# An S4 convolution block with an MLP: four broadcast mask products, inverse sums moved partly to the matmul accumulator, and a new priority table

## The chip, the cores and the metric

The kernel runs on one core of a Trainium2 chip. The metric is device time in microseconds (us) of one execution; lower is better. The engines are named as in the profile: PE is TensorE's matmul path and PEld its weight loads, DVE is VectorE, ACT is ScalarE, POOL is GpSimd, and SP is the engine whose queue issues nearly all DMA transfers.

## What is computed

The reference is a state-space layer (S4) followed by a channel MLP, both with a layer norm in front and a residual around them. Sequence length L is 2048, width D is 512, 128 states per channel, MLP width 1376; inputs and outputs are bf16.

```python
def _A_ref(u, ...):
    dt = jnp.exp(log_dt)[:, None]
    logdA = dt * (A_re + 1j * A_im);  dB = dt * (B_re + 1j * B_im)
    P = jnp.exp(logdA[:, :, None] * l[None, None, :])
    K = jnp.einsum("dn,dnl,dn->dl", Cc, P, dB).real
    # y = irfft(rfft(pad(u)) * rfft(pad(K))), the first L values
    return y + u * Dskip[None, None, :]
def _B_ref(x, ...):
    h = _gelu(jnp.einsum("bsd,df->bsf", _layernorm(x), w1) + b1)
    return jnp.einsum("bsf,fd->bsd", h, w2) + b2
h  = x + _A_ref(_layernorm(x), ...)
h2 = h + _B_ref(_layernorm(h), ...)
```

## The kernel before

**Staging.** The 512 channels are cut into four groups c = 0 to 3 of 128, and the sequence into two halves b = 0 and 1 of 1024 rows. `tables` builds sines and exponentials of the transition for two groups at a time, `kgen` (L1044) forms the convolution kernel's factors from them, and `kspec` (L1074) turns them with the masked weights `W` into one half of the convolution kernel, sends it through DRAM (`AK_d`, 256 KB out and back in) to change its layout, and transforms it (L1112). `ln1` and `xspec` normalise and transform the input; `xswap` makes a copy with the partition halves exchanged. `inverse` (L1118) multiplies spectra and transforms back. For the first half b = 0 a group has one pair (kernel half 0 with input half 0). For b = 1 it has two pairs, since both kernel halves contribute. `tail` (L1216) adds Dskip and the residual and computes the second layer norm's statistics, and `mlp` (L1262) does the two large matmuls (L1274 and L1292) for 512 rows at a time.

**The inverse.** For each of two blocks of eight frequencies (`fh`) and each of two parts `h` (with the matrices `TP1` and `TP2`), a DVE product of 128x1024 bf16 is made for each pair (L1132) into one of four buffers `PR` used in turn. With two pairs the second product is added to the first on DVE (L1134). The resulting `jobs`, always two, go to PE as 8 matmuls of 128x128 each, accumulated in PSUM (L1142), and the sum is evacuated by ACT or DVE (L439 or L441).

**The weights.** `W` has 7 variants of 4 blocks of 128 columns. Each variant and each group g of 32 columns is `valW` (bf16, 4x32) times one column of the mask `msk` (fp32, one value per partition). L830 does this with one `tensor_scalar` of 128 elements for each of the 28 pairs (v, g); the profile shows it as L504, the line of the helper `TS`. `tensor_tensor` calls through the helper `TT` appear as L511. `kspec` reads all of `W`.

**The order of the work.** Nothing is issued in program order. Every step is added to a list with its engine or engines, an estimated cost, and what it reads and writes. `Sched.run` (L192) then plays the list: it repeatedly takes the engine that can start something first, and on it, among the steps that could start within 0.095606 us of the earliest, the one whose group has the smallest number in the table `PRI` (L89; L282). The window and the table thus decide which ready step an engine takes. Groups are named by stage, half and channel group: `iv11` is the inverse of half 1 and group 1, `tl00` and `ty00` are the statistics and the normalised transpose of the first 512 rows, `mu00` and `md00` their two MLP matmuls, `lx0` the second load of the input, which `tail` adds, `cDW` the step that makes `W`. Where a step may run on two engines the plan also chooses the engine. Four PSUM slots of 128x1024 fp32 are shared by all stages and given out by the same plan.

Of the kernel before, what the change touches and what calls it, by code (L numbers as in the profile page):

```python
# [10 lines left out]
ALU = mybir.AluOpType  # L11
# [5 lines left out]
P = 128  # L17
# [60 lines left out]
def runs_of(idx):  # L78
# [8 lines left out]


PRI = {  # L89
    "ta0": 0, "ks03": 1, "gelu": 2, "iv01": 3, "bd02": 4, "dt": 5, "kt00": 6, "iv03": 7, "ty11": 8, "tp": 9, "tl00": 10, "xs11": 11,  # L90
    "gam": 12, "eA": 13, "xs12": 14, "in": 15, "cDW": 16, "bd01": 17, "x10": 18, "iv11": 19, "u0": 20, "kt01": 21, "zt00": 22, "ks11": 23,
    "kt12": 24, "xin1": 25, "x02": 26, "xin": 27, "u1": 28, "c0": 29, "tl10": 30, "xs13": 31, "x03": 32, "xs01": 33, "xs10": 34, "ks10": 35,
    "iv00": 36, "xs00": 37, "ty00": 38, "tb0": 39, "ty10": 40, "x11": 41, "mu00": 42, "cb": 43, "kt03": 44, "eB2": 45, "zt11": 46, "sa": 47,
    "eB": 48, "bd00": 49, "st": 50, "kg2": 51, "w2": 52, "bd10": 53, "zt02": 54, "tl01": 55, "iv13": 56, "mu01": 57, "bd03": 58, "iv10": 59,
    "ks02": 60, "md01": 61, "zt03": 62, "x00": 63, "iv12": 64, "kg3": 65, "lx1": 66, "trig": 67, "sm": 68, "ks01": 69, "kt02": 70, "sinT": 71,
    "kt13": 72, "zt13": 73, "bd13": 74, "tl11": 75, "kt10": 76, "x01": 77, "kg0": 78, "iv02": 79, "mu10": 80, "tb1": 81, "ks00": 82, "lwt": 83,
    "md10": 84, "ks12": 85, "psi": 86, "ty01": 87, "zt01": 88, "w1": 89, "ln1": 90, "ks13": 91, "xs03": 92, "md00": 93, "x13": 94, "bd11": 95,
    "cB": 96, "kg1": 97, "ln0": 98, "cW": 99, "lx0": 100, "x12": 101, "mu11": 102, "bd12": 103, "zt10": 104, "md11": 105, "zt12": 106, "xs02": 107,
    "ta1": 108, "kt11": 109,
}  # L100


# [45 lines left out]
class Sched:  # L148
# [43 lines left out]
    def run(self, nslots):  # L192
# [72 lines left out]
        while av:  # L265
            while wants and ops[wants[0]].start is not None:
                wants.pop(0)
            fs = sorted((slots[s], s) for s in range(nslots) if taken[s] is None)
            best = {}
            for i in av:  # L270
                o = ops[i]
                need = len(o.new)
                if need > len(fs) or (need and i != wants[0] and len(fs) - need < len(ops[wants[0]].new)):
                    continue
                ts = fs[need - 1][0] if need else 0.0
                for e in o.eng:
                    s = max(free[e], ready(o, e), ts)
                    best.setdefault(e, []).append((s, o.pr, i))
            assert best, "stuck"
            e = min(best, key=lambda q: (min(best[q])[0], ENGS.index(q)))  # L280
            s0 = min(best[e])[0]
            s, _, i = min((c for c in best[e] if c[0] <= s0 + 0.095606), key=lambda c: (c[1], c[2]))  # L282
            o = ops[i]
            av.remove(i)
            c = o.cost[o.eng.index(e)] if len(o.cost) > 1 else o.cost[0]
            if e == "PE":
                if o.new:
                    fill(o, max(free[e], fs[len(o.new) - 1][0]), s)
                c = pecost(s, c, o.mm)
            o.start, o.e = s, e  # L290
            free[e] = s + c
            if o.byts:
                b = max(s + c + 1.3, dma_busy)
                dma_busy = b + o.byts / 218e3
                o.end = dma_busy + 0.7
            else:
                o.end = s + c
            for n, p in enumerate(o.new):
                sl = fs[n][1]
                p.slot = sl  # L300
                taken[sl] = p
            for p in set(o.ps):
                left[p] -= 1
                if left[p] == 0:
                    taken[p.slot] = None
                    slots[p.slot] = o.end + LAT_NEXT[e]
            order.append(o)
            for u in users[i]:
                nd[u] -= 1
                if nd[u] == 0:  # L310
                    av.append(u)
# [18 lines left out]
def kernel(ctx, tc, A_u, A_A_re, A_A_im, A_B_re, A_B_im, A_C_re, A_C_im, A_log_dt, A_Dskip,  # L330
# [34 lines left out]
    W = take(bf16, 7, 4, P)  # L365
# [6 lines left out]
    st = take(f32, 8, 6)  # L372
# [11 lines left out]
    psi = take(f32, 512)  # L384
    gam = take(f32, 512)
# [109 lines left out]
    def TS(o, i, s1, s2, op0, op1=None, n=None, mode=2, psum=False, oap=None, iap=None, extra=(), pr=None, eng="DVE"):  # L495
        r = [i] + [s for s in (s1, s2) if isinstance(s, V)] + list(extra)
        f = lambda s: (s.ap() if isinstance(s, V) else s)
        n = n if n is not None else (o.hi - o.lo) // SZ[o.dt]

        def fn(e):  # L500
            a = oap() if oap else o.ap()
            b = iap() if iap else i.ap()
            if op1 is None:
                dve.tensor_scalar(a, b, f(s1), None, op0)  # L504
            else:
                dve.tensor_scalar(a, b, f(s1), f(s2), op0, op1)
        add("DVE", c_dve(n, mode, psum) + 0.065 * sum(isinstance(q, V) for q in (s1, s2)), fn, r=r, w=[o], pr=pr)

    def TT(o, a, b, op, n=None, mode=1, psum=False, oap=None, aap=None, bap=None, pr=None):
        n = n if n is not None else (o.hi - o.lo) // SZ[o.dt]  # L510
        add("DVE", c_dve(n, mode, psum), lambda e: dve.tensor_tensor(oap() if oap else o.ap(), aap() if aap else a.ap(), bap() if bap else b.ap(), op), r=[a, b], w=[o], pr=pr)  # L511
# [131 lines left out]
    msk = ct(f32, 29)  # L643
# [14 lines left out]
    for z in range(2):  # L658
        for r in range(2):
            TT(BD[z], valB, mB, ALU.mult, n=64, oap=lambda z=z, r=r: BD[z].ap().rearrange("p f r g -> p r g f")[:, r], aap=lambda r=r: valB.ap()[:, r].unsqueeze(1).to_broadcast([P, 4, 16]),  # L660
               bap=lambda z=z: mB.ap()[:, 4 * z:4 * z + 4].unsqueeze(2).to_broadcast([P, 4, 16]))
# [163 lines left out]
        TS(DD, valD, mD[g:g + 1], None, ALU.mult, n=32, oap=lambda g=g: DD.ap()[:, :, :, g])  # L825
    valW = ct(bf16, 4, 32)
    AC(valW, codW, ACT.Sin, scale=SINSC, oap=lambda: valW.ap().rearrange("p a b -> p (a b)"), iap=lambda: low16(codW), tbl=True)
    for v in range(7):
        for g in range(4):
            TS(W[v], valW, msk[4 * v + g:4 * v + g + 1], None, ALU.mult, n=128, mode=4, oap=lambda v=v, g=g: W[v].ap()[:, :, 32 * g:32 * g + 32])  # L830

    for f0 in range(0, 16, 4):
        for half, TPx in ((0, TP1), (1, TP2)):
# [284 lines left out]
    def inverse(b, c, pairs, zt, nz):  # L1118

        S.pr = f"iv{b}{c}"  # L1120
        z = Z[nz % 2]
        for fh in range(2):
            f0 = 8 * fh
            p = Ps()
            jobs = []
            for h, TPx in ((0, TP1), (1, TP2)):
                acc = None
                for kf, Xp in pairs:
                    x = Xp[h]
                    pr_ = PR[npr[0] % 4]  # L1130
                    npr[0] += 1
                    add("DVE", c_dve(1024, 2), lambda e, kf=kf, x=x, pr_=pr_, f0=f0: dve.tensor_tensor(pr_.ap(), kf[f0:f0 + 8].ap(), x[f0:f0 + 8].ap(), ALU.mult), r=[kf[f0:f0 + 8], x[f0:f0 + 8]], w=[pr_])  # L1132
                    if acc is not None:
                        add("DVE", c_dve(1024, 2), lambda e, acc=acc, pr_=pr_: dve.tensor_tensor(acc.ap(), acc.ap(), pr_.ap(), ALU.add), r=[acc, pr_], w=[acc])  # L1134
                    else:
                        acc = pr_
                jobs.append((acc, TPx))

            def fn(e, p=p, jobs=jobs, f0=f0):
                for k in range(8):  # L1140
                    for n, (q, TPx) in enumerate(jobs):
                        pe.matmul(pst(p)[:, 128 * k:128 * k + 128], lhsT=q.ap()[:, k, :], rhs=TPx[f0 + k].ap(), start=(n == 0), stop=(n == len(jobs) - 1))  # L1142
            add("PE", 0.44 * len(jobs), fn, r=[q for q, _ in jobs] + [TP1, TP2], w=[p], new=[p], mm=8 * len(jobs))
            evac(lambda z=z, f0=f0: z.ap()[:, :, f0:f0 + 8], lambda p=p: pst(p).rearrange("d (f q) -> d q f", f=8), 1024, [p], [z])
        S.pr = f"zt{b}{c}"
        if b == 1:
            dmat(lambda: zt.ap(), lambda: z.ap().rearrange("d q f -> d (q f)"), [z], [zt])
            return
        p = Ps()

        def tfn(e, p=p):
            for s in range(16):
                pe.transpose(pst(p, bf16)[:, 128 * s:128 * s + 128], z.ap()[:, 8 * s:8 * s + 8, :].rearrange("d q f -> d (q f)"), identb.ap())
        add("PE", 0.88, tfn, r=[z, identb], w=[p], new=[p], mm=16)

        def zfn(e, p=p):
            o, i = zt.ap().rearrange("p s d -> p (s d)"), pst(p, bf16)
            if e == "ACT":
                act.copy(o, i)
            else:  # L1160
                dve.tensor_copy(o, i)
        add(("DVE", "ACT"), (c_dve(2048, 2), c_act(2048)), zfn, r=[p], w=[zt])
# [222 lines left out]
```

## Time and profile before

| what | value |
|---|---|
| median of 8 runs | 279.17 us (277.72 to 283.0) |
| the profiled execution | 279.54 us, of which its span is 277.7 us |
| PE busy | 234.5 us (84% of the span) |
| DVE busy | 210.9 us (76%) |
| ACT busy | 198.5 us (71%) |
| POOL busy | 11.6 us (4%) |
| mean granted PE clock | 0.937 |
| DMA traffic | 30.07 MB |

The span runs from the first to the last instruction of the profiled execution; 1.84 us of that execution's own time lie outside it. Times below are counted from the start of the span. A group row gives the busy time of a group of instructions, the mean duration of one in ns, and the idle time of the engine ahead of them with what ended it. Durations of neighbouring instructions on one engine overlap, so the distance from one start to the next is shorter than a duration.

### The profile page before, as it was taken

The page shows a single profiled execution, that of the slowest core. Times are in us where ns is not written, and L with a number is a line of the kernel's source. Part 1 is how long each engine was busy: PE and PEld are TensorE (multiplying, and loading weights), DVE is VectorE, ACT ScalarE, POOL GpSimd, SP SyncE. Part 2 cuts the span into 40 slices and gives each one's busy share as a digit, 9 for nine tenths or more (in the row PEclk, how much of TensorE's full clock was granted, in tenths as well). Part 3 has the DMA queues.
Part 4 walks back from the last instruction along what each step waited for, and adds up shares of the span by engine and source line. Part 5 has one row for each costly group of instructions (what it writes and reads, how often), then busy time and mean ns, then how long its engine had stood idle before and what let it go on. Part 6 is the DMA issues. An engine that isn't in the chain of part 4 may idle for free.

```text
span 277.7 us, 7867 instructions
## 1 busy us (share of the span) xinstructions
PE 234.5 (84%) x3266; PEld 143.7 (52%) x3282; DVE 210.9 (76%) x499; ACT 198.5 (71%) x230; POOL 11.6 (4%) x136
## 2 busy tenths in 40 slices
PE   6498459688779998759998978679999999999993
PEld 2372124325366754647977865454664444444441
DVE  7899999999964997985669999999970598612011
ACT  2899999989997898145887996998956414841700
POOL 8410000000000000000000000000000000000000
PEclk9999597958999996897999997999999999999999
DMA  6360661043002089878977989976055002002002
GB/s 138 71 152 27 202 170 22 0 130 81 2 2 82 13 156 242 192 197 213 228 189 198 222 190 238 212 181 114 0 105 105 19 21 57 0 2 58 20 24 53
DMA packets 41240, 30.07 MB, mean 108 GB/s; under 512 B 29971, under 2 KB 37492, under 8 KB 40948
## 3 DMA queue, kind: packets, MB, share of 16 engines
q1 hardware_dynamic: 39476, 29.05, 44.3%
q10 hardware_dynamic: 1728, 0.52, 0.9%
q8 instruction: 25, 0.41, 0.6%
q14 instruction: 11, 0.09, 0.1%
HBM read 15.27 MB, written 8.00 MB: 84 GB/s over the span
## 4 chain that ended last, share of the span: by engine, by line
PE 47%; DVE 21%; ACT 18%; issue 6%; DMA 5%; SPq 1%; POOL 0%; DVEq 0%; ACTq 0%; POOLq 0%
PE ps L1292 13%; PE ps L1274 13%; ACT ar L439 5%; DVE ar L441 4%; PE ps L1142 3%; ACT ar L987 3%; PE ps L1058 3%; PE ps L1098 3%; DVE ar L959 3%; DVE ar L504 3%; PE ps L1059 3%; ACT ar L798 3%; DVE ar L511 2%; DMA ar<-AK_d 2%; DVE ar L965 2%
## 5 line engine op out<-in xcount | busy, mean ns | idle before, releaser
L439 ACT CAST ar<-ps 128x1024 bf16<-128x1024 f32 (+2 forms) x67 | 62.7, 986 | 25.2 <-PE ps L1059 8.4
L1276 ACT ACTIVATE ar<-ps,ar 128x512 bf16<-128x512 f32 (+1 forms) x44 | 29.8, 686 | 23.0 <-PE ps L1274 16.6
L1274 PE MATMUL ps<-ar 128*128 128x512 bf16 (+1 forms) x172 | 40.1, 379 | 0.6 <-ACT ar L439 0.3
L1292 PE MATMUL ps<-ar 128*128 128x512 bf16 (+1 forms) x169 | 39.6, 379 | 0.3
L1294 DVE TENSOR_TENSOR ar<-ps,ar 128x512 bf16<-128x512 f32 x16 | 11.0, 690 | 37.2 <-PE ps L1292 37.2
L441 DVE CAST ar<-ps 128x1024 bf16<-128x1024 f32 (+3 forms) x25 | 27.0, 1106 | 10.4 <-PE ps L1059 4.2
L987 ACT ACTIVATE ar<-ps 128x1024 bf16<-128x1024 int16 x36 | 34.3, 1051 | 0.4 <-DVE ar L965 0.4
L1132 DVE TENSOR_TENSOR ar<-ar 128x1024 bf16<-128x1024 bf16 x48 | 31.2, 683 | 0.9 <-PE ps L1142 0.8
L1274 PEld LDWEIGHTS <-ar 128*128 128x128 bf16 (+1 forms) x176 | 17.3, 100 | 20.1 <-issue 0.8
L1292 PEld LDWEIGHTS <-ar 128*128 128x128 bf16 (+1 forms) x176 | 16.9, 98 | 19.1
L511 DVE TENSOR_TENSOR ar<-ar 128x4 f32<-128x4 f32 (+5 forms) x73 | 21.2, 316 | 1.1
L1059 PE MATMUL ps<-ar 128*20 128x33 bf16 x512 | 19.3, 248 | 3.2 <-issue 3.1
L1058 PE MATMUL ps<-ar 128*20 128x33 bf16 x512 | 19.2, 250 | 1.6 <-DVE ar L965 1.3
L1059 PEld LDWEIGHTS <-ar 128*20 128x20 bf16 x512 | 17.6, 126 | 4.3 <-issue 4.3
L1058 PEld LDWEIGHTS <-ar 128*20 128x20 bf16 x512 | 17.1, 124 | 3.7 <-DVE ar L965 1.8
L1142 PE MATMUL ps<-ar 128*128 128x128 bf16 x256 | 16.9, 223 | 1.3 <-ACT ar L439 1.3
L965 DVE TENSOR_TENSOR ar<-ar 128x1024 bf16<-128x1024 bf16 x26 | 17.4, 682 | 0.3
L1142 PEld LDWEIGHTS <-ar 128*128 128x128 bf16 x256 | 15.7, 100 | 3.3 <-issue 0.8
L1031 PE MATMUL ps<-ar 128*32 128x512 f16 x200 | 13.4, 381 | 2.5 <-ACT ar L987 1.3
L1353 PE MATMUL ps<-ar 128*128 128x512 bf16 x28 | 12.3, 566 | 3.7 <-ACT ar L732 2.3
L896 ACT COPY ar<-ps 128x2048 bf16<-128x2048 bf16 x7 | 13.2, 1887 | 2.3 <-PE ps L918 2.3
L1098 PE MATMUL ps<-ar 20*128 20x256 bf16 (+1 forms) x448 | 12.7, 257 | 2.5 <-issue 1.5
(95 smaller groups left out, 370.9 us busy)
## 6 DMA issues: line engine op xcount, KB each, us to landing
AK_d<-ar SPq DMA_DIRECT2D x16, 256.0 KB
ar<-AK_d SPq DMA_DIRECT2D x16, 256.0 KB
ar<-ar SPq DMA_DIRECT2D x16, 256.0 KB
ar<-in_A_u_dram SPq DMA_DIRECT2D x4, 512.0 KB
ar<-in_A_u_dram SPq DMA_DIRECT2D x8, 256.0 KB
out_dram<-ar SPq DMA_DIRECT2D x32, 64.0 KB
ar<-in_B_w_dram SPq DMA_DIRECT2D x4, 344.0 KB
ar<-in_B_w_dram SPq DMA_DIRECT2D x10, 128.0 KB
```

Of the source, the lines that this page charges most:

```text
L439: act.copy(out_fn(), in_fn())
L441: dve.tensor_copy(out_fn(), in_fn())
L511: add("DVE", c_dve(n, mode, psum), lambda e: dve.tensor_tensor(oap() if oap else o.ap(), aap() if aap else a.ap(), bap() if bap else b.ap( ...
L965: add("DVE", c_dve(1024, 2), lambda e: dve.tensor_tensor(ent(e0, lo, 4, rv), ent(e0, lo, 4, rv), Cx(), ALU.mult), r=rE + [sc[1]], w=rE)
L987: add("ACT", c_act(1024), lambda e, p=p, kp=kp: act.activation(sc.ap()[:, :, 2 * kp:2 * kp + 2, :], pst(p).bitcast(i16).rearrange("p (k s ...
L1058: pe.matmul(o, lhsT=Ar.ap()[:, :, d], rhs=Br.ap()[:, :, d], start=True, stop=False, tile_position=(0, 32 * g))
L1059: pe.matmul(o, lhsT=Ai.ap()[:, :, d], rhs=Bi.ap()[:, :, d], start=False, stop=True, tile_position=(0, 32 * g))
L1132: add("DVE", c_dve(1024, 2), lambda e, kf=kf, x=x, pr_=pr_, f0=f0: dve.tensor_tensor(pr_.ap(), kf[f0:f0 + 8].ap(), x[f0:f0 + 8].ap(), ALU. ...
L1142: pe.matmul(pst(p)[:, 128 * k:128 * k + 128], lhsT=q.ap()[:, k, :], rhs=TPx[f0 + k].ap(), start=(n == 0), stop=(n == len(jobs) - 1))
L1274: pe.matmul(pst(p)[:fs, 512 * z:512 * z + 512], lhsT=w1s[dc].ap()[:, fc * P:fc * P + fs], rhs=ybuf.ap()[:, dc, :], start=(dc == 0), stop=( ...
L1276: add("ACT", c_act(512, 1), lambda e, p=p, z=z, fc=fc, fs=fs: act.activation(hT.ap()[:fs, fc, :], pst(p)[:fs, 512 * z:512 * z + 512], ACT. ...
L1292: pe.matmul(pst(p)[:, 512 * z:512 * z + 512], lhsT=hT.ap()[:fs, fc, 128 * t:128 * t + 128], rhs=w2s[fc].ap()[:fs], start=(fc == 0), stop=( ...
```

## The change

Three things are changed.

The 28 scalar products that make `W` become four broadcast products, one for each of the four column blocks `tl`: `valW[tl]` is broadcast over variants and groups, and the mask over the 32 columns, with 896 elements in each.

In `inverse`, the sum over pairs stays on DVE only for the groups c = 2 and 3. For c = 0 and 1 each product becomes a job of its own. For b = 1 this gives four jobs in place of two, and so 32 matmuls in place of 16 in each block of eight frequencies; the DVE additions are not issued. For b = 0 there is one pair, and nothing changes.

The priority table is replaced by another one for the same 110 groups, and the window goes from 0.095606 to 0.084764 us. Some of the entries, before and after: `ty00` 38 and 11, `tl00` 10 and 20, `iv10` 59 and 43, `iv11` 19 and 36, `iv12` 64 and 59, `iv13` 56 and 7, `iv00` 36 and 85, `iv01` 3 and 81, `iv02` 79 and 88, `iv03` 7 and 4, `lx0` 100 and 2, `mu00` 42 and 73, `cDW` 16 and 14, `tb0` 39 and 55.

```diff
-            s, _, i = min((c for c in best[e] if c[0] <= s0 + 0.095606), key=lambda c: (c[1], c[2]))
+            s, _, i = min((c for c in best[e] if c[0] <= s0 + 0.084764), key=lambda c: (c[1], c[2]))
...
-    for v in range(7):
-        for g in range(4):
-            TS(W[v], valW, msk[4 * v + g:4 * v + g + 1], None, ALU.mult, n=128, mode=4, oap=lambda v=v, g=g: W[v].ap()[:, :, 32 * g:32 * g + 32])
+    for tl in range(4):
+        TT(W, valW, msk, ALU.mult, n=896, oap=lambda tl=tl: W.ap()[:, :, tl].rearrange("p v (g i) -> p v g i", g=4),
+           aap=lambda tl=tl: valW.ap()[:, tl].unsqueeze(1).unsqueeze(1).to_broadcast([P, 7, 4, 32]),
+           bap=lambda: msk.ap()[:, 0:28].rearrange("p (v g) -> p v g", v=7).unsqueeze(3).to_broadcast([P, 7, 4, 32]))
...
+            summed = c >= 2
...
-                    if acc is not None:
+                    if not summed:
+                        jobs.append((pr_, TPx))
+                    elif acc is not None:
                         add("DVE", c_dve(1024, 2), lambda e, acc=acc, pr_=pr_: dve.tensor_tensor(acc.ap(), acc.ap(), pr_.ap(), ALU.add), r=[acc, pr_], w=[acc])
                     else:
                         acc = pr_
-                jobs.append((acc, TPx))
+                if summed:
+                    jobs.append((acc, TPx))
```

## The prediction

> **What bounds the kernel now.** I read the busy slices first, then a table of stretches, then the order of instructions on DVE and PE where the edits fall. Slices (40 of 6.94 us; each digit is tenths busy):
>
> ```profile
> PE   6498459688779998759998978679999999999993
> DVE  7899999999964997985669999999970598612011
> DMA  6360661043002089878977989976055002002002
> ```
>
> DVE is full from 14 to 76 us and again from 146 to 201 us. PE is full from 187 us to the end. DMA is mostly busy from 97 to 187 us. So different engines set the pace in turn. The table of stretches (columns: stretch and its length, then PE, PEld, DVE, ACT and POOL busy, PE clock, DMA share, GB/s) shows the change-over:
>
> ```profile
> 160.00:170.00 10.00, 8.35 (x148) 6.32 (x146) 10.00 (x16) 8.24 (x8) 0.00 (x0) 0.88 0.88 202
> 170.00:184.50 14.50, 9.41 (x122) 7.69 (x121) 13.63 (x39) 13.35 (x16) 0.00 (x0) 0.97 0.99 211
> 184.50:206.00 21.50, 21.25 (x167) 12.77 (x171) 21.36 (x53) 18.21 (x23) 0.00 (x0) 1.00 0.45 90
> 206.00:240.00 34.00, 33.84 (x193) 16.01 (x195) 21.44 (x65) 15.78 (x23) 0.00 (x0) 1.00 0.21 45
> ```
>
> From 184.5 us, where the first MLP matmul (L1274) starts, PE has 0.25 + 0.16 us of idle time in 55.5 us. From there on, each microsecond of PE work is a microsecond of time. Just before, PE is idle for 14.50 - 9.41 = 5.09 us: there PE work can be hidden, or the MLP can start earlier.
>
> The inverses that change stand in this order on PE (start, duration, instruction, idle time ahead in brackets):
>
> ```profile
> 169.61 1.68 PE L1142 MATMUL ps<-ar 128*128 128x128 bf16 x16
> ...
> 174.27 0.61 PE L1112 MATMUL ps<-ar 128*128 128x128 bf16 x8 [0.31 <-ACT ar L439]
> 175.19 1.05 PE L1142 MATMUL ps<-ar 128*128 128x128 bf16 x16 [0.31 <-ACT ar L439]
> ...
> 179.39 0.61 PE L1112 MATMUL ps<-ar 128*128 128x128 bf16 x8 [1.02 <-DMA ar<-AK_d]
> ...
> 181.09 1.05 PE L1142 MATMUL ps<-ar 128*128 128x128 bf16 x16 [0.65 <-ACT ar L439]
> ...
> 184.54 1.02 PE L1274 MATMUL ps<-ar 128*128 128x512 bf16 x3 [0.31 <-ACT ar L439]
> 185.45 1.05 PE L1142 MATMUL ps<-ar 128*128 128x128 bf16 x16
> ```
>
> In the order of issue the first two blocks belong to channel group 0 of the second half and the next two to group 1; groups 2 and 3 come at 194.11, 198.49, 202.21 and 206.79 us. Three of the four blocks that grow lie in the stretch with gaps, one in the full one.
>
> **What the Trainium skill says.** "VectorE: DVE Perf Modes", section on the TRN2 errata, prices an SBUF operation at 58 + elements/mode cycles of 0.96 GHz, and its section on the perf-mode tier table keeps `tensor_tensor` with fp32 at one element per cycle. For 896 elements that is an estimate of 954/0.96 = 994 ns, and the trace agrees: the 928-element fp32 product that also reads a broadcast operand starts at 35.72 us and the next instruction at 36.74. For the small scalar products the same rule gives 58 + 128/4 = 90 cycles, 94 ns; the trace shows 163 ns, and I take that. "TensorE: Matmul & The Clock Gate", section "Wait — 56ns, not 53.3ns?", gives 55.6 ns for a 128-column matmul on a warm clock and 106.7 on a cold one. The trace agrees: 16 at 185.56 us on the chain take 0.94, and 0.89 in the blocks from 194 us on.
>
> **Mask products.** The group by shape and the DVE order:
>
> ```profile
> L504 DVE TENSOR_SCALAR ar<-ar 128x128 bf16<-128x128 bf16 x28 | 5.0, 245 | 0.0
> L511 DVE TENSOR_TENSOR ar<-ar 128x928 f32<-128x928 f32 x1 | 1.1, 1108 | 0.0
> ```
>
> Of the 28, 24 run in one row from 56.53 us for 3.98 us, so one takes (3.98 - 0.24)/23 = 0.163 us, and all 28 take 4.55. The four new ones at (1.02 us for 928 elements, less 32 at about 1 ns) 0.99 take 3.95. The saving is 0.60 us. DVE has no idle time from 50.3 to 80.5 us and the chain runs through these instructions at 56.6 and 58.8 us, so I count all of it. The unknown is that both operands are broadcast, one along its innermost dimension. The 1728-element product, which has both forms of broadcast, takes 1.95 us including its tail, or 1.13 ns an element: at that price four cost 4.05, saving 0.5. If the plan places a whole 0.99 us block ahead of something urgent, where a 0.163 us one fitted a gap, the edit loses up to 0.8 each, 3 in all; if the replaced ones had also held up `gam`, it gains up to 1.1.
>
> **Inverse sums.** Removed: two additions in each of four blocks, eight at a start-to-start 0.60 us (two take 1.29 with the last one's tail, from 204.97 us), 4.8 us of DVE:
>
> ```profile
> L1134 DVE TENSOR_TENSOR ar<-ar 128x1024 bf16<-128x1024 bf16 x16 | 10.6, 686 | 0.0
> L1142 PE MATMUL ps<-ar 128*128 128x128 bf16 x256 | 16.9, 223 | 1.3 <-ACT ar L439 1.3
> ```
>
> Added: 16 matmuls in each block, 64 x 0.0556 = 3.56 us of PE. At a cold clock this would be up to 64 x 0.107 = 6.8, but the stretch has a clock of 0.97. All eight removed additions lie before 184.6 us, at 163.45 (two), 172.16, 173.70, 177.60, 180.01 and 183.34 (two). What do they hold up? The path to the first MLP matmul: the residual (L1234, 165.86), the statistics (171.88 to 177.63, many small steps) and the normalise step (L1249, 180.61). The pair at 163.45 stands ahead of the residual, but PE delivers at 165.25, so at most 0.6 is lost there; the two inside the statistics cost 1.2; those at 177.60 and 180.01 stand ahead of the last normalise step, 1.2. Up to 3.0 us of earlier MLP start are there, which would help only as far as PE has idle time to give up.
>
> The new waits: a block now reads all four product buffers, so the first product of the next block waits for 32 matmuls rather than 16, with all of DVE's queue behind it. The profile shows 0.8 us of such waits in two places. The bound is 4 x 0.89 = 3.6 on DVE, less than the 4.8 that it gives back, and I cost it at nothing. It would cost what the statistics lose if they stand behind it. The PSUM slot is also held 0.89 longer by each block; that is part of the PE sum.
>
> **The new order.** In favour: `ty00` now stands ahead of `iv11` (11 against 36, before 38 against 19), so the normalise steps pass the products. Against: `iv00` and `iv01` fall to 85 and 81, behind `x10` and `x11` of the second half, though the first MLP part needs them. `mu00` falls behind all inverses of the second half; PE is full, so the order costs nothing there. `lx0` goes from 100 to 2, and its four DMA issues of 256 KB can pass others on SP's queue. With the window below the plan's hand-over times, the table decides only among steps ready together, so I take the net of it as zero and put its two ends into the rivals.
>
> **The sum.** PE's additional 3.56 us count in full where PE is full, and in the stretch ahead as far as its gaps don't take them. Of the 5.09 us of gaps, five of 0.31 to 0.33 (1.57 us) are hand-overs after an ACT eviction that recur whatever is queued; 3.52 remain. With new work and an earlier MLP competing for these, I take half: 1.76. So 3.56 - 1.76 - 0.60 = +1.20. On the profiled execution's 279.54 (span 277.7 and 1.84 around it) that is 280.74; the median of the runs is 0.37 lower, so **280.4**. Its own range is 279.9 (most gaps used) to 282.1 (no gap used: +2.96).
>
> **Rivals.** All come from the same profile; a measurement of this kernel can tell about 0.3% (0.84 us) from no change.
>
> *Faster: the relief starts the MLP earlier.* DVE was the bound ahead of the MLP, 23.63 of 24.5 us busy from 160 to 184.5. Without additions in the statistics, and with `ty00` ahead, the MLP starts 3 us earlier and all the gaps are used: 3.56 - 5.09 - 0.60 = -2.1, so 277.0. It decides if more than about 3.8 of the 5.09 us vanish. Against it: gaps after ACT evictions and the 1.02 us wait for `AK_d` are not DVE's. Chance 0.31.
>
> *Cancelled:* gaps filled to 2.2 to 3.8 us, total within 0.84 of before, 279.2. Chance 0.15.
>
> *Clearly slower: DMA order.* DMA is 0.99 busy until 184.5. If the four loads of `lx0` (1.05 MB at 211 GB/s, 5.0 us) pass the `AK_d` transfers that the inverses need, the MLP starts 5.0 later; of the new PE work only the block after the start remains (0.89): 5.0 + 0.89 - 0.60 = +5.3, so 284.5. Lower ranks of `iv00` and `iv01` would do the same. Against: most loads start when their buffers come free, not when they rank. Chance 0.19.
>
> My forecast has 0.35 and is slower. So slower has 0.35 + 0.19 = 0.54, same 0.15, faster 0.31. The range goes from 276.0 (the faster case, with 1.1 for the masks rather than 0.6, and 0.5 of gaps after 160) to 285.0 (the DMA case, with the masks at no gain).
>
> **What would show it.** Four `tensor_tensor` of 896 elements at about 1 us. L1134 with 8 instances, L1142 with 320 matmuls. PE busy up by some 3 to 4 us, DVE down by about 5. The start of L1274: at 183 to 184 by my forecast, with PE work after it near 0.9 to 1.8 longer; at 181 or before in the faster case; beyond 187 with a wait for DMA ahead in the slow one. I am wrong if PE before the MLP start shows other stages moved by several us, since I set the new order at zero.

## The result and the profile after

| what | before | after |
|---|---|---|
| median | 279.0 us (32 runs, 277.34 to 283.0) | 282.22 us (11 runs, 280.65 to 286.84) |
| the profiled execution, and its span | 279.54 us, 277.7 us | 283.22 us, 281.0 us |
| start of the first `kgen` matmul | 81.29 us | 86.53 us |
| start of the first MLP matmul | 184.54 us | 185.68 us |
| end of the last group, `md11` | 274.2 us | 277.5 us |
| mean granted PE clock | 0.937 | 0.95 |

After divided by before is 1.0111, with an interval of 1.0083 to 1.0139: the change costs 3.1 us (2.3 to 3.9). The forecast was +1.2. Some executions of both kernels fall in a slower state (the 283.0 and the 286.84 of the table); the ratios and intervals here compare the others. The inserted lines shift the numbering: L1132 is now L1134, L1142 is L1147, L1274 is L1279, L1058 is L1059, L987 is L988, L918 is L919, L926 is L927. In kernels with only one of the edits the shift is smaller.

The page's busy slices of the kernel after (40 of 7.03 us):

```profile
PE   6787667789778697669998897799999999999993
DVE  7899997988974988797679999989990498603011
DMA  6264440016000229899978799839245002002002
```

Two things differ from the slices of before. DVE is no longer full from 14 to 76 us: digits of 7 and 8 stand among the 9s from the seventh on. And the row of 9s that ends PE's line begins one slice earlier, at the 27th, and yet the span is 3.3 us longer. The table of stretches for the kernel after, with the columns explained in the prediction:

```profile
160.00:170.00 10.00, 9.83 (x249) 8.63 (x247) 9.31 (x14) 8.17 (x9) 0.00 (x0) 1.00 1.00 228
170.00:184.50 14.50, 10.71 (x134) 8.61 (x132) 13.95 (x41) 10.59 (x10) 0.00 (x0) 0.90 0.89 207
184.50:206.00 21.50, 21.34 (x201) 14.09 (x202) 20.24 (x49) 17.72 (x23) 0.00 (x0) 0.99 0.48 104
206.00:240.00 34.00, 33.79 (x205) 16.46 (x207) 22.09 (x53) 15.17 (x21) 0.00 (x0) 1.00 0.27 57
```

The gaps ahead of the MLP are smaller: 14.50 - 10.71 = 3.79 us where there were 5.09. Behind 184.5 us PE is as full as before. The two groups of the inverse, and the blocks on PE, show the edit as foretold, 320 matmuls and no additions (two views, the groups and the order on PE; the second of the four blocks, at 175.44 us, is broken by a wait into 3 and 29 matmuls and left out):

```profile
L1147 PE MATMUL ps<-ar 128*128 128x128 bf16 x320 | 21.0, 224 | 0.7 <-DVE ar L1134 0.3
L1134 DVE TENSOR_TENSOR ar<-ar 128x1024 bf16<-128x1024 bf16 x48 | 31.3, 683 | 1.3 <-PE ps L1147 1.0
```

```profile
168.35 2.01 PE L1147 MATMUL ps<-ar 128*128 128x128 bf16 x32
...
182.99 2.85 PE L1147 MATMUL ps<-ar 128*128 128x128 bf16 x32
...
185.68 1.89 PE L1279 MATMUL ps<-ar 128*128 128x512 bf16 x7
...
190.47 1.95 PE L1147 MATMUL ps<-ar 128*128 128x128 bf16 x32
```

L1147 has 21.0 us where L1142 had 16.9, which is 4.1 for the 3.56 of the forecast. One block took 2.85 instead of 1.95, for most of it at half the clock (181.5 to 184.9 us). The 48 instances of L1134 are products; before, products and additions shared two groups, so the forecast's "8 instances" named only the additions that remain and not the row that the page would show.

So far this could be read as "3.56 us of matmuls, mostly not hidden". The chain of waits in order of time says otherwise. The first matmul of `kgen` before, and then after:

```profile
81.29 0.27 PE ps L1058 x4
```

```profile
86.53 0.28 PE ps L1059 x4
```

The kernel after is 5.2 us late at this point, 80 us ahead of the first inverse that changed. It is still 5.2 late when `ln1`, the layer norm of the input's second half, starts (116.4 against 111.2), 3.8 at the last transpose of the first half (164.9 against 161.1), 1.1 at the first MLP matmul, and 3.3 at the end. The 5.2 is not the loss itself: the second and third groups of `kgen` are only 2.6 and 3.2 us late (93.9 against 91.3, and 114.9 against 111.7).

### The profile page after: what moved, and what is told of

It reads as the page before. It is cut to its first block, busy times and chain, and to the rows that moved or that the text cites. A ratio compares the mean times of both kernels' runs of the same rounds, so it can differ in the third digit from the quotient of the medians.

```text
span 281.0 us, 7958 instructions
## 1 busy us (share of the span) xinstructions
PE 237.6 (85%) x3324; PEld 148.3 (53%) x3339; DVE 208.9 (74%) x473; ACT 192.4 (68%) x224; POOL 11.5 (4%) x136
## 4 chain that ended last, share of the span: by engine, by line
PE 48%; DVE 11%; issue 6%; ACT 4%; DVEq 0%; ACTq 0%
PE ps L1297 13%; PE ps L1279 13%; PE ps L1147 5%; PE ps L1059 4%; PE ps L1060 3%; DVE ar L441 3%; PE ps L1099 3%; PE ps L1113 2%; PE ps L1234 2%; ACT ar L988 2%; DVE ar L1134 1%; DVE ar L966 1%; PE ps L1261 1%; DVE ar L1166 1%; DVE ar L1239 1%
## 5 line engine op out<-in xcount | busy, mean ns | idle before, releaser
L439 ACT CAST ar<-ps 128x1024 bf16<-128x1024 f32 (+2 forms) x65 | 61.3, 978 | 27.6 <-PE ps L1060 9.8
L1279 PE MATMUL ps<-ar 128*128 128x512 bf16 (+1 forms) x171 | 40.2, 379 | 0.3
L988 ACT ACTIVATE ar<-ps 128x1024 bf16<-128x1024 int16 x36 | 34.6, 1050 | 3.2 <-DVE ar L966 1.7
L441 DVE CAST ar<-ps 128x1024 bf16<-128x1024 f32 (+3 forms) x27 | 29.4, 1114 | 8.6 <-PE ps L1060 3.2
L1134 DVE TENSOR_TENSOR ar<-ar 128x1024 bf16<-128x1024 bf16 x48 | 31.3, 683 | 1.3 <-PE ps L1147 1.0
L1279 PEld LDWEIGHTS <-ar 128*128 128x128 bf16 (+1 forms) x176 | 17.1, 100 | 19.5 <-issue 0.4
L1297 PEld LDWEIGHTS <-ar 128*128 128x128 bf16 (+1 forms) x176 | 16.9, 98 | 19.1
L511 DVE TENSOR_TENSOR ar<-ar 128x4 f32<-128x4 f32 (+5 forms) x77 | 25.5, 352 | 1.3 <-ACT ar L523 0.2
L1059 PE MATMUL ps<-ar 128*20 128x33 bf16 x512 | 19.9, 250 | 6.7 <-issue 5.3
L1060 PEld LDWEIGHTS <-ar 128*20 128x20 bf16 x512 | 18.0, 126 | 7.2 <-issue 7.2
L1147 PE MATMUL ps<-ar 128*128 128x128 bf16 x320 | 21.0, 224 | 0.7 <-DVE ar L1134 0.3
L1147 PEld LDWEIGHTS <-ar 128*128 128x128 bf16 x320 | 19.5, 101 | 2.9 <-issue 0.8
L1060 PE MATMUL ps<-ar 128*20 128x33 bf16 x512 | 19.9, 248 | 0.8 <-issue 0.8
L1059 PEld LDWEIGHTS <-ar 128*20 128x20 bf16 x512 | 17.5, 124 | 3.4 <-DVE ar L966 2.5
L897 ACT COPY ar<-ps 128x2048 bf16<-128x2048 bf16 x6 | 11.2, 1873 | 5.8 <-PE ps L919 5.8
L1000 PE MATMUL ps<-ar 65*32 65x512 f16 x128 | 11.5, 448 | 3.7 <-ACT ar L988 1.7
L965 DVE TENSOR_TENSOR ar<-ar 128x512 bf16<-128x512 bf16 x26 | 10.0, 421 | 6.1 <-ACT ar L988 3.2
```

Of the source, the lines that this page charges most:

```text
L439: act.copy(out_fn(), in_fn())
L441: dve.tensor_copy(out_fn(), in_fn())
L988: add("ACT", c_act(1024), lambda e, p=p, kp=kp: act.activation(sc.ap()[:, :, 2 * kp:2 * kp + 2, :], pst(p).bitcast(i16).rearrange("p (k s ...
L1059: pe.matmul(o, lhsT=Ar.ap()[:, :, d], rhs=Br.ap()[:, :, d], start=True, stop=False, tile_position=(0, 32 * g))
L1060: pe.matmul(o, lhsT=Ai.ap()[:, :, d], rhs=Bi.ap()[:, :, d], start=False, stop=True, tile_position=(0, 32 * g))
L1279: pe.matmul(pst(p)[:fs, 512 * z:512 * z + 512], lhsT=w1s[dc].ap()[:, fc * P:fc * P + fs], rhs=ybuf.ap()[:, dc, :], start=(dc == 0), stop=( ...
```

## The theories

*Order* (called A in the expectations; A1 is its narrow form, that the two x-transform groups `x00` and `x01` alone do it): the new order of the steps ahead of `kgen` costs the time, and neither edit of instructions does. *Edits* (C in the expectations; it is what the prediction's sum states): the 64 matmuls cost it. *Masks* (B): a mask block of 1 us holds up the phase steps `gam` that the sines wait for. *DVE* (D): from 50 to 80 us DVE sets the pace, so what leaves it there comes back as time. Against D stands P: the sines on ACT and the PSUM slots set the pace there, and DVE only fills in. P' is a later attempt, that sines ahead of the evacuations on ACT bring `kgen` forward.

In the names of groups, `tb0` and `ta0` are the first tables (8 and 10 sines of 128x1024), `tb1` begins the second ones, and `bd` and `x` are the two parts of `xspec`: a first matmul, then the transposes and the x transform. An evacuation is a copy from PSUM by ACT or DVE.

Since the table decides the order of everything, one edit under the old table gives a wholly different plan. So in each experiment the order is written out and replayed. It names the step, its engine and its PSUM slots. "Old" and "new" below mean the order of before and of after, cut at 92.5 us of the plan's time, which is past the start of the second `kgen` group. An order fixes the engines too: in the early part of after, 16 evacuations stand on the other of ACT and DVE than in before, eight each way, so "the order" means both. The ratios compare each kernel with runs of before from the same session; the trace of before is from a session of its own. The medians of before went from 278.06 to 279.0 us between sessions, so about 1 us between traces of two sessions proves nothing. Every experiment has this edit:

```diff
-    order = S.run(NSL)
+    order = replay(S, NSL)
```

| kernel | order up to 92.5 | order from there | masks | inverses of groups 0 and 1 | time / before |
|---|---|---|---|---|---|
| w_in_old_order | old | old | four products | sums | 1.0036 (1.0012 to 1.006) |
| inv_in_old_order | old | old | 28 | jobs | 1.0361 (1.0314 to 1.0409) |
| early_new | new | old | 28 | sums | 1.0153 (1.0088 to 1.0218) |
| late_new | old | new | 28 | jobs | 1.002 (0.9998 to 1.0042) |
| early_new_x_late | new, `x00`, `x01` later | old | 28 | sums | 1.0459 (1.0373 to 1.0545) |
| mid_new | old to 46, then new | old | 28 | sums | 1.0418 (1.0318 to 1.0517) |
| after_mask_late | new, masks later | new | four | jobs | 1.0107 (1.0038 to 1.0175) |
| after_sums | new | new | four | sums | 1.0298 (1.0218 to 1.0378) |
| masks_in_gap | old, masks later | old | four | sums | 0.999 (0.9958 to 1.0021) |
| masks_in_gap_late_new | old, masks later | new | four | jobs | 1.0006 (0.9972 to 1.0041) |
| after_masks_gap | new, masks later | new | four | jobs | 1.0326 (1.0257 to 1.0394) |
| masks_in_gap_sines | old, masks and sines moved | old | four | sums | 1.0179 (1.013 to 1.0229) |

## The change taken apart

**The masks alone, in the old order** (w_in_old_order). The edit is the diff's second part, the four products standing where the last 24 small ones stood.

> The order of the kernel before is written out step by step; only the 28 small mask products are replaced by the four broadcast ones, each in the place of the last of seven. Theory A (the loss comes from the order of the steps ahead of the first kernel-generation matmuls): -0.6 us against before, since DVE saves 28 x 0.163 - 4 x 0.99 there and has no idle time. Rival B (the broadcast products, 1 us each, hold up the phase steps and with them the tables): +2 us or more, and the first kernel-generation matmul starts later than 81.3 us. Rival C (the added matmuls): says as A for this run.

Measured: 1.0036 (1.0012 to 1.006), 278.94 us, or +1.0 us. Part of the answer is in the group by shape on DVE, from 50 to 62 us of this kernel:

```profile
L511 DVE TENSOR_TENSOR ar<-ar 128x896 bf16<-128x896 bf16 x4 | 4.1, 1085 | 0.0
```

The four together occupy DVE from 56.28 to 60.37 us, 4.09, and the 24 small ones that they replace took 3.98, from 56.53. The other four small ones had stood between the steps of a dependent chain and cost 0.15 us: the seven steps ahead of the row take 3.38 us without them (from 52.90) and 3.53 with them (from 53.00). So nothing was there to save. But a saving of nothing is not a loss of 1.0: the first `kgen` matmul is at 81.2 us, as in before. The traces come from different sessions, so a loss of 1 us can't be followed from one to the other, and it stays open.

**The inverses alone, in the old order** (inv_in_old_order). The edit is the diff's third part. The additions are left out of the order, and each engine keeps its order but for two steps of the residual on DVE, which go ahead of two products.

> The order of the kernel before is written out; only the eight additions of groups 0 and 1 are taken out and their products go to PE as jobs of their own (two small statistics steps pass a product, since it now waits for 32 matmuls). Theory A: between -0.5 and +1.8 us; my forecast's own sum for this part alone was +3.56 - 1.76 = +1.8. Rival C (all added PE work counts): +3.0 to +3.6 us. Rival B: about 0.

Measured: 1.0361 (1.0314 to 1.0409), 288.58 us. The waits of this kernel from 158 to 190 us show it (total, times, longest):

```profile
DVE ar L1133 <- PE ps L1146: 12.3, 3, 5.7
```

and the stretch from 160 to 184.5 us:

```profile
160.00:184.50 24.50, 15.62 (x231) 12.88 (x229) 13.64 (x38) 14.59 (x14) 0.00 (x0) 0.86 0.66 152
```

A product for the next block stands on DVE ahead of the rest of the residual and the statistics, and waits until PE has read one of the four buffers, 5.7 us in the longest case. That rest of the residual (L1238 in this kernel) runs behind it, and PE's next group waits 3.66 us for that, up to 175.03 us. So DVE, which was 23.63 of 24.5 us busy here, is 13.64 busy, and the first MLP matmul starts at 192.0 us. In the order of after the same wait (the 1.0 us in the row of L1134 above) is nearly nothing. The edit and the late part of the order belong together. The 3.6% is thus the price of the edit in an order that was made for the additions.

**The late part together** (late_new: the inverse edit with the order of after from 92.5 us on), and **the early part alone** (early_new: only the order up to there, not one instruction changed).

> 28 mask products and the order of before up to 92.5 us of the plan; from there the order of the kernel after and its inverse sums (groups 0 and 1 summed by PE). Theory A: -1.5 us (-2.5 to -0.5), since the kernel after is 5.0 us behind at its second layer norm and 3.3 at the end. Rival B: about 0. Rival C: +3 us.

> Old code (28 mask products, all sums on DVE). The steps up to 92.5 us of the plan, which reach past the start of the second kernel-generation group, stand in the order of the kernel after; all later steps stand in the order of before. Theory A: +4 us (3 to 5), the first kernel-generation matmul near 86.5 us rather than 81.3, and nothing made up later. Rivals B and C: within 1 us of before, since neither edit is in it.

Measured: late_new 1.002 (0.9998 to 1.0042), +0.6 us; early_new 1.0153 (1.0088 to 1.0218), +4.3 us (2.4 to 6.1). This is the pair that decides: a loss as large as that of the change (the intervals overlap) comes with an order that touches neither edit. The first `kgen` matmul of early_new is as late as that of after:

```profile
86.83 0.28 PE ps L1058 x4
```

The parts add up to more than the whole, 4.3, 0.6 and the masks' 1.0 against 3.1; the intervals leave room for that. In late_new the same stretch as above reads

```profile
160.00:184.50 24.50, 20.13 (x327) 16.08 (x325) 23.95 (x54) 18.11 (x19) 0.00 (x0) 1.00 0.87 200
```

PE does 20.13 us of work there instead of 17.76, and its order shows where the MLP now starts:

```profile
180.28 1.95 PE L1146 MATMUL ps<-ar 128*128 128x128 bf16 x32 [0.31 <-ACT ar L439]
182.06 1.89 PE L1278 MATMUL ps<-ar 128*128 128x512 bf16 x8
```

The first MLP matmul comes 2.5 us earlier than in before, and the last group ends at 273.9 us where it ended at 274.2. This start varies by itself: in masks_in_gap below, whose late part is that of before, it is at 181.62, in one of its shortest executions. But masks_in_gap_late_new, of the same session, has it at 179.36, again 2.3 us earlier. That is the faster rival's mechanism at work, about enough to pay for the 3.56 us of matmuls.

**The sums put back in the order of after** (after_sums).

```diff
-            summed = c >= 2
...
-                    if not summed:
-                        jobs.append((pr_, TPx))
-                    elif acc is not None:
+                    if acc is not None:
...
-                if summed:
-                    jobs.append((acc, TPx))
+                jobs.append((acc, TPx))
```

> The kernel after with its own order and masks, but the eight additions of groups 0 and 1 are put back on DVE, each right behind its second product, and PE sums two jobs again. My forecast's sum (the edit costs 3.56 - 1.76): 1.8 us faster than after, +1.3 against before. Rival (DVE is the bound ahead of the MLP in this order, so the edit gains there): slower than after by 1 us or more, +4.

Measured: 1.0298 (1.0218 to 1.0378), 287.5 us. With the additions back on DVE, each behind its products, the kernel loses 1.9 points more than after does. In the new order, which was made for the edit, the inverse edit is worth some 5 us. The cost of the change isn't the price of the 64 matmuls.

## Where the early order loses its time

ACT works through sines, which `kgen` needs, and through evacuations of PSUM. The groups of ACT over the 18 sines of `tb0` and `ta0`, in before (51.45 to 78.15 us; the copy ahead of the first sine is in it) and in after (51.75 to 84.45 us):

```profile
L987 ACT ACTIVATE ar<-ps 128x1024 bf16<-128x1024 int16 x18 | 17.3, 1041 | 0.4 <-DVE ar L965 0.4
L439 ACT CAST ar<-ps 128x1024 bf16<-128x1024 f32 x5 | 4.9, 1021 | 1.4 <-PE ps L910 1.4
L896 ACT COPY ar<-ps 128x2048 bf16<-128x2048 bf16 x2 | 3.7, 1863 | 0.0
```

```profile
L988 ACT ACTIVATE ar<-ps 128x1024 bf16<-128x1024 int16 x18 | 17.8, 1035 | 0.6 <-DVE ar L966 0.5
L439 ACT CAST ar<-ps 128x1024 bf16<-128x1024 f32 x9 | 9.1, 1019 | 1.2 <-PE ps L911 0.8 <-PE ps L927 0.4
L897 ACT COPY ar<-ps 128x2048 bf16<-128x2048 bf16 x2 | 3.7, 1867 | 1.8 <-PE ps L919 1.8
L523 ACT ACTIVATE ar<-ar 128x32 f32<-128x32 int16 (+1 forms) x2 | 0.4, 258 | 0.0
```

After has nine evacuations (L439) instead of five, 4.2 us more, and 3.6 us of idle time instead of 1.8. The last sine of `ta0` ends 6.3 us later, 84.6 against 78.3. Counted from the end of the table load instead, it is ten against seven, and the load itself starts 1.6 us later, with one more evacuation just ahead of it (47.73). early_new, which has neither edit, shows nine as well, and late_new five:

```profile
L439 ACT CAST ar<-ps 128x1024 bf16<-128x1024 f32 x9 | 9.1, 1019 | 1.5 <-PE ps L910 0.8 <-PE ps L926 0.7
```

```profile
L439 ACT CAST ar<-ps 128x1024 bf16<-128x1024 f32 x5 | 4.9, 1022 | 1.4 <-PE ps L910 1.4
```

The idle time is new at L919, the x transform, on which ACT waits. That is a chain between two engines: PE's next matmuls for the sines stand behind an x transform and its evacuation. On PE in after, from 57 to 64 us:

```profile
57.61 1.89 PE L919 MATMUL ps<-ar 128*128 128x128 bf16 x16
59.29 1.06 PE L911 MATMUL ps<-ar 128*128 128x256 bf16 x4
61.45 1.93 PE L927 MATMUL ps<-ar 128*128 128x128 bf16 x16 [1.10 <-ACT ar L897]
63.31 1.90 PE L1000 MATMUL ps<-ar 65*32 65x512 f16 x16
```

L1000 makes the arguments of the sines of `tb0`. In before the last eight of these matmuls start at 60.96 us; here the last sixteen stand behind L927, which waits for the copy L897 on ACT. By this reading, what was moved in this stretch is work for ACT, and ACT has no time to give: from 66 to 80 us it is 13.63 of 14 us busy in before. Part of it comes from DVE. Between the table load and the last sine ACT has twelve evacuations in after (L439 and L897), of which six stand on DVE in before, the three of `x03` among them; of the nine in before, four stand on DVE in after. No run puts back the engines alone. Not all of the time is lost for good: the moved evacuations don't have to be done later (ACT is busy for 45.78 us from 90 to 160 us in after, for 50.21 in before). This may be part of why the 5.2 us have become 1.1 at the MLP; the earlier start of the MLP with the new late order, 2.3 to 2.5 us, may be the other part.

The stretches of 52 to 80 us, for before and for after:

```profile
52.00:66.00 14.00, 10.88 (x99) 5.82 (x96) 14.00 (x50) 12.56 (x14) 0.30 (x2) 0.63 0.40 104
66.00:80.00 14.00, 11.14 (x165) 5.98 (x162) 13.97 (x22) 13.63 (x15) 0.00 (x0) 1.00 0.01 2
```

```profile
52.00:66.00 14.00, 11.47 (x104) 6.66 (x102) 12.86 (x25) 12.06 (x13) 0.67 (x2) 0.61 0.20 62
66.00:80.00 14.00, 11.19 (x149) 7.43 (x148) 12.66 (x21) 12.38 (x13) 0.07 (x1) 0.90 0.19 44
```

DVE and ACT have time to spare in after that they didn't have in before, and PE runs at half its clock for longer: 55.2 to 68.9 us instead of 54.9 to 65.1. One could put the loss down to that clock. after_sums speaks against it: the same early order, with half clock for only 6.8 us between 50 and 85 us (10.2 in before), has its first `kgen` matmul at 86.2.

**Is it the masks?** (after_mask_late: the kernel after, with the four mask products put behind the last step of `gam` on DVE.)

> The kernel after with its own order, but the four mask products stand behind the last phase step (gam) on DVE rather than three of them between its steps. Rival B: about 3 us faster than after, so near before, since the phase steps end at 58 us rather than 61.4. Theory A1: within 1 us of after (+3 us against before), since the table products stand behind both on DVE.

Measured: 1.0107 (1.0038 to 1.0175), as after. The first `kgen` matmul is at 87.0 us. B falls.

**Is it the position of `x00` and `x01`?** (early_new_x_late: early_new, with these two groups behind the first step of `kg0` on each engine.)

> As early_new, except that the transforms of the input's channel groups 0 and 1 (x00 and x01: transposes, matmuls and their evacuations by ACT and DVE) stand behind the first kernel-generation group rather than ahead of the tables; nothing else is moved. Theory A1 (the new table puts input transforms ahead of the table steps on ACT, DVE and PE): the first kernel-generation matmul comes back to about 83 us from 86.8, and the total to within +2 us of before. Rival B (the mask products delay the phase steps and through their DMA the second tables): no gain against early_new, +4 us.

Measured: 1.0459 (1.0373 to 1.0545), 292.09 us. What A1 foretold did not come. Six evacuations are left on ACT between 52 and 84 us, the three of `x03` not being among those moved, but the first `kgen` matmul is only 0.8 us earlier than in early_new, at 86.0, and the second group `kg1` is 8 us later, at 102.3. ACT spends 5.6 us idle between 52 and 84 us, mostly behind PE, and PE has half its clock for 27.3 us between 53.0 and 90.6. The seam has its own waits, so the run does not clear `x00` and `x01`; it does show that fewer evacuations on ACT are not enough to bring `kgen` forward.

**Is it what happens before 46 us?** The trigonometric table load starts at 48.86 us in after and 47.27 in before, so 1.6 of the 5.2 us is older than this stretch. mid_new has the old order to 46 us and goes on with early_new's.

> As early_new, but the steps up to 46 us of the plan (setup, exponentials) stand as before and only those from 46 to 92.5 us as in the kernel after. Theory A1: +3 us against before, since the loss arises between the sine table's load and the first kernel-generation matmul. Rival (the setup's order, which puts the load of the sine table 1.6 us later): +1 us or less.

Measured: 1.0418 (1.0318 to 1.0517). The load starts at 47.1 us, but behind the seam ACT is only 6.83 of 14 us busy from 52 to 66, PE has half its clock from 52.1 to 76.0 us, and the first `kgen` matmul is at 94.3. The seam is itself a bad order, and the run tells nothing about the 1.6 us: inconclusive.

## Looking for something better

If DVE sets the pace from 50 to 80 us (D), the four mask products should move to where it is idle, behind `ta0`. In masks_in_gap they stand at 80.80, 81.81, 84.88 and 85.88 us. For this the mask and the weights get a place of their own, since the fifth sine writes over theirs:

```diff
-    msk = ct(f32, 29)
+    ct(f32, 29); msk = at(y2s[0].lo, f32, 29)
-    valW = ct(bf16, 4, 32)
+    ct(bf16, 4, 32); valW = at(y2s[1].lo, bf16, 4, 32)
```

> The kernel before with its order and its inverses, but the masks as four broadcast products that stand behind the last product of the first tables on DVE (two) and behind the next evacuation (two), where DVE waits from 80.5 to 84.1 and from 85.3 to 87.5 us. For that the mask and the weights have to live in a buffer of their own, since the sine tables overwrite their place from the third group on. Theory D (DVE is the bound from 50 to 80 us, so what stands there counts, in number and not only in form): up to 3.9 us faster than before (28 x 0.163 less what fell in gaps), at least 2. Rival P (the tables are paced by ACT's sines and by PSUM slots there, DVE is full because it fills in): within 1 us of before.

> masks_in_gap up to 92.5 us of the plan, then the order of after with its inverse sums. late_new against before was +0.2%. Theory D: as masks_in_gap, within 1 us. Rival P: as late_new, +0.5 us against before.

> The kernel after, with the four mask products behind the last product of the first tables (own buffer as above) and eight table products ahead of the evacuation of x02 on DVE, which PE delivers only at 62.4 us. Theory D: the table products start near 58 us rather than 63.7, and the total comes 3 us or more below after, so to before or better. Rival P: within 1.5 us of after; the first kernel-generation matmul stays near 86 us, since PE order and PSUM slots hold the sines.

Measured: 0.999 (0.9958 to 1.0021), 1.0006 (0.9972 to 1.0041) and 1.0326 (1.0257 to 1.0394). The stretches of masks_in_gap:

```profile
52.00:66.00 14.00, 10.59 (x88) 5.78 (x88) 11.40 (x24) 12.45 (x14) 0.20 (x1) 0.64 0.38 104
66.00:80.00 14.00, 11.44 (x171) 6.45 (x168) 12.87 (x19) 13.91 (x15) 0.00 (x0) 0.99 0.01 2
```

DVE was relieved of 2.6 + 1.1 us, and ACT, 13.91 of 14 us busy, did the same sines at the same time: the one behind the evacuation starts at 60.66 us, at 60.80 in before. The first `kgen` matmul is at 80.9 instead of 81.3. DVE was full and did not set the pace; D falls, and P's forecast came. That also shows why the masks' price hardly mattered. With the order of after (after_masks_gap, where the first products of `tb0` also go ahead of an evacuation on DVE) half clock lasts from 56.4 to 80.3 us and `kgen` starts at 92.1.

The last attempt puts four sines ahead of evacuations on ACT, in masks_in_gap (masks_in_gap_sines).

> As masks_in_gap, and on ACT the fifth to eighth sine groups of the first tables stand ahead of the evacuations of bd00 and bd03 that they stood behind (the fifth had to wait for the masks before, since it overwrites their constants; it no longer has to). Theory P' (ACT sets the pace between the sine table's load and the first kernel-generation matmul, so only its idle time and the order of its work count): the idle 1.2 us ahead of bd00 at 58.6 us goes, the first kernel-generation matmul starts at 79 to 80 us rather than 80.9, and the total is 1 to 2 us below before. Rival (the waits ahead of the second tables, for the phase's transfer through DRAM and for DVE, take up what is gained): within 0.8 us of before.

Measured: 1.0179 (1.013 to 1.0229). Its stretches:

```profile
52.00:66.00 14.00, 11.37 (x84) 6.03 (x83) 11.39 (x24) 12.55 (x14) 0.20 (x1) 0.54 0.39 104
66.00:80.00 14.00, 10.29 (x127) 5.67 (x128) 8.97 (x15) 11.33 (x12) 0.00 (x0) 0.74 0.01 2
```

The sines came early and the evacuations late. PE waited for ACT 6.3 us from 53 to 85 us, against 5.4 in masks_in_gap, half clock lasted from 53.1 to 70.1 and from 77.0 to 83.8 us, and ACT, which was to gain, was 11.33 of 14 us busy instead of 13.91. None of these versions is faster than before by more than its interval.

What is shown is that the new early order costs the time and that it comes with more evacuations and more waiting on ACT ahead of the sines. That these cause the loss is read from the traces and not shown by a run. Which single move of that order costs how much is open too, and so is the share of the engines chosen for the evacuations: the two attempts to undo a part of it, early_new_x_late and mid_new, made a worse order of the rest.

## Why the prediction was right or wrong

- **Sign and range.** Slower, as forecast; 282.22 lies in the range of 276.0 to 285.0, and 0.1 above the forecast's own range. The size was 2.6 times the forecast, and the cause is mostly not the one that it named. That sign and range came out right is luck: the matmuls with their late order cost 0.6 us where the sum had 1.8, and most of the loss comes from a term set at zero.
- **"I take the net of it as zero"** (the new order). This is the step that failed. Alone, the order up to `kgen` costs 4.3 us. The argument was that the table only decides among steps ready together. But the 110 new ranks changed the early order on every engine, with four more evacuations among the sines on ACT, which was nearly full there, and the last sine of `ta0` 6.3 us later. The prediction looked at the order only near its edits, and at the ranks of groups there; the 110 ranks were all new, and the stretch from 45 to 90 us was not priced. Its own last sentence ("other stages moved by several us") names what was found.
- **PE work +3.56, of which 1.76 absorbed.** The work is right (4.1 us on the page, of which 0.9 for one block at half clock). Absorption was too small: late_new costs 0.6 (-0.1 to 1.2) in all, so about 3.0 of the 3.56 are absorbed, in the new late order. The reason is the faster rival's: with the old early order the MLP starts 2.3 to 2.5 us earlier. The forecast used gaps and no earlier start.
- **Masks -0.60.** The price of a block is right: 1.00 us from start to start, with 0.994 estimated from the Trainium skill, "VectorE: DVE Perf Modes", section on the TRN2 errata. What they replace was mis-sized. 28 times 0.163 counts four instructions that stood between dependent steps and cost 0.15 in all; the 24 in a row took 3.98, so the saving is within 0.1 of nothing. The run with this edit alone even took 1.0 us longer (0.3 to 1.7), for a reason that stays open. And masks_in_gap shows that even the whole 4 us was not on the path: 0.999.
- **The new buffer waits, at nothing.** Right in the order of after, 1.0 us; in the old order the same waits are 12.3 us and the run 3.6% longer. The statement "what the statistics lose if they stand behind it" was the correct alternative.
- **The start of L1274 at 183 to 184, with 0.9 to 1.8 more work after it.** It was 185.68, and from there to the end of the last group after takes 91.8 us where before took 89.7: 2.1 more. The 0.9 that a block lost at half clock lies ahead of this start and is part of its delay.
- **The DMA rival.** Not the cause: late_new has the new rank of `lx0` and of `iv00`, `iv01`, and costs 0.6.
- **The faster rival.** Its mechanism is there and gives 2.3 to 2.5 us; the early order takes more.

## What to carry to other kernels

When a change comes with a new priority table, the table is the change: compare the order of the whole program, engine by engine, and price first the stretch where the most engines are full, even if no edit is near it. An instruction on a full engine is worth its time only if that engine sets the pace; moving it to a gap is a cheap trial, and here it gave nothing. An edit that lengthens how long a buffer is held is to be judged with the order that it will run in: the same edit cost 3.6% in an order made without it and gained about 1.9% in one made with it.

## What was not expected of the hardware

- Two broadcast operands, one along its innermost dimension, cost a `tensor_tensor` of 896 elements nothing beyond its size: 1.00 us from start to start, against 1.02 for the plain 928 elements with one broadcast operand.
- PE fell to half its clock at 54.9 us in before, although the longest idle time on it between 46.7 and 55 us was 1.15 us; it was only busy for 3.07 of the 5 us ahead. The Trainium skill, "TensorE: Matmul & The Clock Gate", Part 1, section "What's actually happening", says that the clock is set by activity windows of about 3.4 us and goes to half after an idle one. The lengths agree: but for the last one of a run, which its end cuts off, the half-clock stretches of all these runs are 3.4, 6.8, 10.2, 13.7, 17.1, 23.9 or 27.3 us, steps of 3.4. But a window with gaps of 1.15 us at most was enough here.
- Orders of the same work differ by up to 4.6% in time, and the longest half-clock stretches between 50 and 95 us (17 us and more in a row, or 27.3 in three parts) stand in the four kernels of the table that put new seams into the early order. Ahead of 50 us such stretches did no harm to `kgen`: late_new has 23.9 us of them there, before 10.2, and the first `kgen` matmul is at 81.2 and 81.3. That more waiting brings half clock, and half clock more waiting, fits this; no run separates the two.
